# Offsets modulo 256 bytes of the matmul operands in a fused attention and MLP kernel

## The chip, the cores and the metric

The kernel runs on one core of a Trainium2 chip. The metric is the device time of one execution in microseconds (us). Of the kernel before there are three runs: 1198.25, 1200.48 and 1200.82 us, with a median of 1200.48 us.

## The reference

The input x has 2048 rows of 576 columns. It is normalised row by row (layer norm without weights), and three terms are added:

```python
xn = layernorm(x)
qkv = xn @ wqkv                      # 576 x 1728: 32 heads of 18
# each row attends to 8 keys: itself and 7 earlier rows, 2 apart
attn = softmax(q . k[idx] * 18**-0.5, masked where idx < 0)
A = (attn . v[idx]) @ wo             # 576 x 576
B = relu(xn @ w1) @ w2               # w1 576 x 4608, w2 4608 x 576
out = x + A + B
```

All of it is float32.

## The kernel before, in words

**Precision.** [...] Each operand is split into a high part (a rounded copy, ScalarE) and a low part (the rest, VectorE; `hi_lo`, line 278), and high times high, high times low and low times high are summed in PSUM. So each weight and activation tile has a high and a low half.

**Work and order.** The rows are taken in two phases of 1024 rows (`NPH`), each in two halves h of 512 rows. In a phase the 4608 columns of w1 are passed in 18 steps of 256; a step m has its own set of weights, and a half of a step is a unit g. Each unit computes h = relu(w1-columns x xn) for 512 rows and adds h times the rows of w2 to the outputs.

- *First product* (`classic`, line 583, and `pstep`, line 605): the weights of w1 (`wset`) are the stationary operand, 128 x 128, and the activations `xa`, `xs` (sums and differences of row blocks, in a scheme that saves one of eight block products) and `xr` (the last 64 rows of the contraction) the moving one, 256 wide, into the PSUM banks `bk2`, `bk3` and `bkA`. The steps P1 to P7 of a unit have six or eight matmuls each.
- *Output product* (`o_step`, line 720): 128 columns of `hhi` or `hlo` are the stationary operand and a row block of w2 (`w2t`) the moving one, in two pieces: 256 and 320 wide. Six matmuls, three pairs of 256 and 320, make one row block. The bank is `po`. The same function multiplies the turned attention output (`ohi`, `olo`) by wo; that tile comes from the pool `v`, whose two slots also hold the attention's values.
- *QKV* (`qkv_tile`, line 778): 14 matmuls a tile with the activations as stationary and a weight tile of 3 x 144 = 432 columns as moving operand, into `pm`. It uses the free one of the two weight buffers.

All matmuls but the transposes are issued in one helper (line 276), ScalarE's copies in another (line 270), VectorE's sums in a third (line 273). While one matmul streams its moving operand, the weights of the next are loaded from SBUF; the profile has the loads in a row of their own (PEld).

**Attention** runs on VectorE in the background, eight heads at a time, between the operations that TensorE waits for. The attention output is turned by way of DRAM.

**What sets the order.** The order of all instructions is written by the program: a planner (`Order`, line 55) keeps a clock for each engine, gives each ScalarE and VectorE operation a length and a due time, and issues the most urgent one that is ready. It knows nothing of addresses. Loads from DRAM are issued on SP's queue (`send`), with margins of some microseconds (`w2_make`, line 491: 4.0); copies of the weights within DRAM go on POOL's queue.

**Where tiles lie.** Each tile has 128 partitions; its offset in a partition follows from the order of the pools and of the tiles in them, each tile rounded up to 32 bytes. The pools are, in order, `keep` (the tiles that live for the whole run, the two weight buffers `BUF` among them), `w2p` (w2), `hp` (h), `whp` (turned attention output), `vp` (values and wo), `prp`, `lgp`, `smp` and `mvp` (scratch of attention and normalisation). A weight buffer has 10 x 432 floats, 17280 bytes. `wset` (line 247) cuts it into a high and a low half, 8640 bytes apart; `wqset` (line 251) into ten parts of 1728 bytes.

Of the kernel before, what the change touches and what calls it, by code (L numbers as in the profile page):

```python
# [9 lines left out]
F32 = mybir.dt.float32  # L10
F32R = mybir.dt.float32r
# [5 lines left out]
P = 128  # L17
NPH = 2
NI = 8
TBN = 256  # L20
W = 8
HG = 8
NU = 4
KT = 4
# [4 lines left out]
WOP = ((6, 9, 13, 16), (7, 10, 14, 17))  # L29
HALO = ((0, 112), (112, 127))  # L30
WARM = 24

S2, S4, S3, S1 = range(4)
T1, B11, T2, B21, T3, B22, T4, RR = range(8)
# [18 lines left out]
class Order:  # L53
# [82 lines left out]
    def act(self, fn, n, after, slack, lag=0.0):  # L136
        op = Op(ACT, n / 1120.0 + 0.06, fn, after, self.now() + slack, lag)
        self.wait[ACT].append(op)
        return op

    def dve(self, fn, n, after, slack, lag=0.0):
        op = Op(DVE, n / 960.0 + 0.062, fn, after, self.now() + slack, lag)
        self.wait[DVE].append(op)
        return op
# [6 lines left out]
    def send(self, fn, kb, after=(), margin=0.0):  # L151

        after = [a for a in after if a is not None]
        self.force(after)
        start = max([self.clk[SP], self.now() - 0.5] + [a.end for a in after])
        fn()
        op = Op(SP, 0.45, None, (), 0.0)
        self.clk[SP] = start + 0.45
        self.dma = max(self.dma, start + 0.3) + kb / 185.0
        op.end = max(start + 2.1, self.dma + 1.2) + margin  # L160
        return op
# [9 lines left out]
    def pe(self, fn, dur, after=()):  # L171
        after = [a for a in after if a is not None]
        self.force(after)
        start = max([self.clk[PE]] + [a.end for a in after])
        while self.step(start):
            pass
        fn()
        op = Op(PE, dur, None, (), 0.0)
        self.clk[PE] = start + dur
        op.end = start + dur + TAIL[PE]  # L180
        return op
# [8 lines left out]
def tile_body(ctx: ExitStack, tc: tile.TileContext, x, wqkv, wo, w1, w2, out):  # L190
# [4 lines left out]
    UD = HG * Dh  # L195
# [9 lines left out]
    ctx.enter_context(tc.manual_schedule())  # L205
    pool = lambda name, bufs, **k: ctx.enter_context(tc.tile_pool(name=name, bufs=bufs, **k))
    keep = pool("keep", 1)
    w2p = pool("w2p", 4)
    hp = pool("hp", 5)
    whp = pool("whp", 2)  # L210
    vp = pool("vp", 2)
    prp = pool("prp", 2)
    lgp = pool("lgp", 1)
    smp = pool("smp", 2)
    mvp = pool("mvp", 8)
    dram = pool("dram", 1, space=bass.MemoryType.DRAM)
    psp = pool("psp", 1, space=PSUM)

    f32 = lambda ap: ap.bitcast(F32)
# [10 lines left out]
    XA = [[keep.tile([P, 2, KT, TBN], F32R, name=f"xa{h}{j}") for j in range(2)] for h in range(2)]  # L230
    XS = [keep.tile([P, 2, 4, 2, TBN], F32R, name=f"xs{h}") for h in range(2)]
    XR = [keep.tile([P, 3, TBN], F32R, name=f"xr{h}") for h in range(2)]
    BUF = [keep.tile([P, 10 * 3 * UD], F32R, name=f"wset{b}") for b in range(2)]
    KK = keep.tile([P, W - 1 + NI, UD], F32, name="kk")
    TS = keep.tile([P, 4, 2, P], F32, name="ts")
    VV = {}
# [7 lines left out]
    bk3 = psp.tile([P, 512], F32, name="bk3")  # L244
    pm = psp.tile([P, 512], F32, name="pm")

    def wset(m):
        z = BUF[m % 2].rearrange("p (e c) -> p e c", e=2)[:, :, 0:2048]
        return z.rearrange("p e (s k c) -> p e s k c", s=8, k=2)

    def wqset(p):
        return BUF[(p + 1) % 2].rearrange("p (t c) -> p t c", t=10)

    def raw_view(z):
        v = z.rearrange("p w c -> p (w c)")[:, 0 : 8 * TBN].rearrange("p (j s k c) -> p j s k c", j=2, s=2, k=2)
        return [v[:, 0], v[:, 1]]

    KR = [raw_view(KK), raw_view(KK)]
    rr = [z.rearrange("p i c -> p (i c)")[:, 0 : 2 * TBN].rearrange("p (j c) -> p j c", j=2) for z in QO]
    RD = [rr[0][:, 0], rr[1][:, 0]]  # L260

    for _ in range(WARM):
        nc.tensor.transpose(po[0][:, 0, 0:P], ident, ident)
# [5 lines left out]
    def copy(o, i, func=AF.Copy):  # L269
        nc.scalar.activation(o, i, func)  # L270

    def sub(o, a, b, op=ALU.subtract):
        nc.vector.tensor_tensor(o, a, b, op=op)  # L273

    def mm(o, l, r, start, stop):
        nc.tensor.matmul(o, l, r, start=start, stop=stop, skip_group_check=True)  # L276

    def hi_lo(hi, lo, raw, n, after, slack):

        a = act(lambda: copy(hi, raw), n, after, slack)  # L280
        b = dve(lambda: sub(lo, raw, f32(hi)), n, [a], slack + 0.8)
        return [a, b]
# [60 lines left out]
    def place(i):  # L343
        return i // 4, i // 2 % 2, slice(i % 2 * P, (i % 2 + 1) * P)
# [68 lines left out]
    def slots_free(b, slots):  # L413
        f = SETFREE.get(b, {})
        return [f[q] for q in slots if q in f]
# [8 lines left out]
    def set_make(m, plain=False, fine=False):  # L424

        n = m % NP
        late = 0.0 if plain or fine or m == 2 else 4.0
        w = wset(m)
        z = f32(w)[:, 1]
        got = {}  # L430
# [65 lines left out]
    WQOK = {}  # L496

    def wq_make(p, u, kts, raw=None):

        w = wqset(p)  # L500
        b = (p + 1) % 2
        v = wqkv.rearrange("r (s c) -> r s c", s=3)[:, :, u * UD : (u + 1) * UD] if raw is not None else WQC[u]
        for kt in kts:
            z = raw[:, kt] if raw is not None else f32(w)[:, 5 + kt]
            after = [] if raw is not None else [kept["wq", u]]
            free = slots_free(b, range(432 * kt // 256, min(7, (432 * kt + 431) // 256) + 1))
            if raw is None:
                after += free
            z3 = z.rearrange("p (s c) -> p s c", s=3)
            if kt < KT:  # L510
                g = [send(lambda: nc.sync.dma_start(z3, v[kt * P : (kt + 1) * P]), 221, after)]
            else:
                g = [send(lambda rows=rows: nc.sync.dma_start(z3[rows], v[KT * P : D]), 110, after)
                     for rows in (slice(0, DR), slice(DR, P))]
            WQOK.setdefault(p, []).extend(hi_lo(w[:, kt], w[:, 5 + kt], z, 3 * UD, [*g, *free], 2.5))

    WO, WOOK = {}, {}

# [259 lines left out]
    def qkv_tile(p, u, i):  # L778
        ph = p // NP
        if i == 0:  # L780
            o_.force(KFREE[0])
            VV[u % 2] = vp.tile([P, W - 1 + NI, UD], F32, name="v")
            nc.gpsimd.memset(KK[0:1, 0 : W - 1, :], 0.0)
            nc.gpsimd.memset(VV[u % 2][0:1, 0 : W - 1, :], 0.0)
        k, v, q = KK, VV[u % 2], QO[u % 2]
        h, j, c = place(i)
        xa, wq = XA[h][j], wqset(p)
        o = pm[:, 0 : 3 * UD]
        lst = (
            [(xa[:, 0, kt, c], kt) for kt in range(KT)] + [(xa[:, 1, kt, c], kt) for kt in range(KT)]  # L790
            + [(XR[h][:, j, c], 4)] + [(xa[:, 0, kt, c], 5 + kt) for kt in range(KT)] + [(XR[h][:, j, c], 9)]
        )

        def f():
            for z, (l, b) in enumerate(lst):
                mm(o, l, wq[:, b], z == 0, z == len(lst) - 1)

        t = pe(f, 14 * 0.196, [*WQOK[p], *XOK[h, j], *BANK["pm"]])
        pq = o.rearrange("p (s c) -> p s c", s=3)

        def out_():
            copy(k[:, W - 1 + i, :], pq[:, 1])
            copy(v[:, W - 1 + i, :], pq[:, 2])
            copy(q[:, i, :], pq[:, 0])

        e = act(out_, 3 * (UD + 70), [t, *OFREE[u % 2]], 1.2)
        BANK["pm"] = [e]
        SETFREE[(p + 1) % 2] = {q: t for q in range(8)}
# [9 lines left out]
    def attention(ph, u, halo):  # L818
        qo, k, v = QO[u % 2], KK, VV[u % 2]
        heads = "p w (h d) -> p w h d"  # L820
        s = {}
        pr = {}

        def begin():
            s["lg"] = lgp.tile([P, NI, W, HG], F32, name="lg")
            s["m"] = smp.tile([P, NI, HG], F32, name="m")
            s["r"] = smp.tile([P, NI, HG], F32, name="r")

        def spread(z):
            return z[:, :, None, :].to_broadcast([P, NI, W, HG])  # L830
# [87 lines left out]
        for i in range(0, NI, 2):  # L918
            for f in (qk_mul, qk_sum):
                for j in (i, i + 1):  # L920
                    z = add(lambda f=f, j=j: f(j), big, halo if first else (), 1.3 if f is qk_sum and j == NI - 1 else 0.0)
# [26 lines left out]
    for m in range(2, NPH * NP):  # L948
        g = 2 * m - 2
        p = m - 1  # L950
# [15 lines left out]
    for ph in range(NPH):  # L966
        for u, n in enumerate(QP[ph]):
            p = ph * NP + n
            g = 2 * p
# [8 lines left out]
        for u, n in enumerate(WOP[ph]):  # L978
            g = 2 * (ph * NP + n)
# [59 lines left out]
        RAWR.pop(h, None)  # L1039

    def x_home(h):
        KR[h] = raw_view(vp.tile([P, W - 1 + NI, UD], F32, name="v") if h else KK)

    for h in range(2):
        g = GP - 1 + h
        at(g - 1, 0, x_home, h)
        at(g - 1, 0, clear, h)
        w = (
            ((33, 14), (33, 15), (33, 16), (33, 17)), ((34, 1), (34, 3), (34, 5), (34, 7)),
            ((34, 8), (34, 10), (34, 14), (34, 16)), ((34, 12), (34, 18)),  # L1050
        ) if h == 0 else (
            ((34, 13), (34, 15), (34, 19), (34, 20)), ((34, 20), (34, 22), (35, 1), (35, 2)),
            ((35, 3), (35, 5), (35, 9), (35, 11)), ((35, 7), (35, 13)),
        )
# [21 lines left out]
    def x_first(i, q=None):  # L1076
        XLAST[i] = send(lambda: (q or nc.sync).dma_start(X[i], x_v[0, i]), 295)

    x_first(0)
    x_first(1, nc.scalar)  # L1080
    VV[0] = vp.tile([P, W - 1 + NI, UD], F32, name="v")
    ST0 = VV[0].rearrange("p w c -> p (w c)")[:, 0:1280].rearrange("p (s k c) -> p s k c", s=5, k=2)
    RAWS = ((B11, 0, 0), (B21, 256, 0), (RR, 512, 0), (B12, 0, 1), (B22, 256, 1))
    SETOK[0] = {}
# [24 lines left out]

    KFREE[0] = WQOK[0]  # L1110
    OFREE[0] = [*W2OK[0, 0], *W2OK[0, 1]]
    KR[0] = raw_view(vp.tile([P, W - 1 + NI, UD], F32, name="v"))
    KR[1] = [
        QO[1].rearrange("p i c -> p (i c)")[:, 0 : 4 * TBN].rearrange("p (s k c) -> p s k c", s=2, k=2),
        TS.rearrange("p s k c -> p (s k c)").rearrange("p (s k c) -> p s k c", s=2, k=2),
# [64 lines left out]
    for g in range(2, NG + 1):  # L1180
        ph, n, h = G[g] if g < NG else (NPH, 0, 0)
# [58 lines left out]
```

## Time and profile before

| | before |
|---|---|
| runs, median of three | 1200.48 us |
| the profiled execution | 1201.66 us |
| its span, first to last instruction | 1199.9 us |
| mean granted TensorE clock | 0.990 |
| instructions | 21930 |
| VectorE busy in the stretch of 500 us from 660 us on | 356.82 us |
| TensorE busy in the same stretch | 496.15 us |
| bytes read and written in DRAM | 96.01 and 36.50 MB |

The span runs from the first to the last instruction of the profiled execution; the time of the execution has 1.8 us more around it. A busy time is the time in which at least one instruction of the engine was under way. Matmuls overlap, so their mean duration is longer than the time from one start to the next. In a group's row stand the line of the code, the engine, the operation, what is written and read, the shape, the count, then the busy time, the mean duration in ns and the idle time before it with its cause. A row of the timeline has the start, the length, the engine, and how many instructions were merged.

### The profile page before, as it was taken

The numbers are of one execution on the slowest core, as the hardware profiler recorded it, in microseconds if no ns is written. First come the engines' busy times: TensorE is split into PE (matmuls) and PEld (weight loads), VectorE is DVE, ScalarE is ACT, GpSimd is POOL, SyncE is SP. The second block draws the span as 40 slices with busy tenths as digits, with TensorE's granted clock in tenths as the row PEclk, the third lists the DMA queues.
The fourth block names the chain that finished last, engine by engine and source line by source line (L and its number), as shares of the span: only waits on it lengthen the run. The fifth ranks groups of instructions, "written<-read, shape, count | busy, mean of one in ns | idle before, by whom it ended". The sixth has DMA issues, their size and how long they took to land.

```text
span 1199.9 us, 21930 instructions
## 1 busy us (share of the span) xinstructions
PE 1162.5 (97%) x8528; PEld 1140.0 (95%) x8528; DVE 826.4 (69%) x1533; ACT 743.0 (62%) x1658; POOL 64.2 (5%) x97
## 2 busy tenths in 40 slices
PE   7999999999988999999999999999999999999998
PEld 6899999999988999899999999999999999999998
DVE  7648978953988169774683299589925994399731
ACT  5548466655656466566686567476646665566663
POOL 2200200110011001000010000000000000000000
PEclk8999999999999999899999999999999999999999
DMA  6752441562245232333352222231322213221322
GB/s 197 218 139 69 150 106 56 161 170 84 68 148 158 42 92 83 120 78 88 120 173 93 71 66 58 44 103 44 89 54 85 71 52 72 83 59 56 80 66 89
DMA packets 133544, 115.60 MB, mean 96 GB/s; under 512 B 54128, under 2 KB 112240, under 8 KB 133120
## 3 DMA queue, kind: packets, MB, share of 16 engines
q1 hardware_dynamic: 128192, 85.00, 25.7%
q0 software_dynamic: 5104, 28.90, 7.5%
q8 instruction: 67, 1.10, 0.4%
q14 instruction: 37, 0.30, 0.1%
q10 hardware_dynamic: 144, 0.29, 0.1%
HBM read 96.01 MB, written 36.50 MB: 110 GB/s over the span
## 4 chain that ended last, share of the span: by engine, by line
PE 73%; DVE 12%; ACT 8%; issue 3%; DMA 3%; POOL 0%; SPq 0%; ACTq 0%; DVEq 0%; POOLq 0%
PE po L276 32%; PE bk L276 21%; PE pm L276 14%; PE bkA L276 5%; DVE wset L273 3%; ACT po L270 2%; ACT x L270 2%; DVE ts L273 2%; DMA olo<-turned 1%; DVE hlo L554 1%; ACT wset L270 1%; DVE sn L273 1%; ACT hhi L270 1%; DVE pr L870 1%; DVE pr L840 1%
## 5 line engine op out<-in xcount | busy, mean ns | idle before, releaser
L276 PE MATMUL po<-w2t,hhi 128*128 128x256 f32 (+1 forms) x2304 | 407.1, 299 | 6.1 <-ACT po L270 5.9
L276 PEld LDWEIGHTS po<-w2t,hhi 128*128 128x128 f32 x2304 | 341.0, 190 | 10.9 <-ACT po L270 9.7
L276 PE MATMUL po<-w2t,hlo 128*128 128x256 f32 (+1 forms) x1152 | 248.1, 297 | 0.0
L276 PE MATMUL bk<-xs,wset 128*128 128x256 f32 x1632 | 238.2, 282 | 7.0 <-DVE sn L273 7.0
L270 ACT ACTIVATE x<-po 128x576 f32<-128x576 f32 x286 | 182.2, 644 | 100.3 <-PE po L276 97.6
L276 PEld LDWEIGHTS bk<-xs,wset 128*128 128x128 f32 x1632 | 217.7, 189 | 8.1 <-DVE sn L273 7.8
L276 PEld LDWEIGHTS po<-w2t,hlo 128*128 128x128 f32 x1152 | 195.7, 191 | 0.0
L270 ACT ACTIVATE po<-x 128x576 f32<-128x576 f32 x286 | 187.0, 654 | 2.9
L276 PE MATMUL pm<-wset,xa 128*128 128x432 f32 x768 | 172.9, 360 | 2.6 <-ACT wset L270 1.5
L276 PEld LDWEIGHTS pm<-wset,xa 128*128 128x128 f32 x768 | 140.2, 188 | 9.9 <-ACT qo L270 2.3
L276 PE MATMUL bk<-xa,wset 128*128 128x256 f32 x924 | 138.7, 288 | 7.5 <-DVE hlo L554 4.8
L273 DVE TENSOR_TENSOR sn<-bk,sn 128x256 f32<-128x256 f32 x136 | 57.2, 421 | 122.0 <-PE bk L276 81.2
L276 PEld LDWEIGHTS bk<-xa,wset 128*128 128x128 f32 x924 | 125.8, 193 | 13.2 <-DVE hlo L554 10.1
L273 DVE TENSOR_TENSOR w2t<-w2t 128x576 fp32r<-128x576 f32 (+1 forms) x72 | 54.1, 751 | 70.1 <-ACT w2t L270 69.4
L270 ACT ACTIVATE hhi<-sn 128x256 fp32r<-128x256 f32 x136 | 56.4, 415 | 72.7 <-DVE sn L273 72.7
L270 ACT ACTIVATE kk<-pm 128x144 f32<-128x144 f32 (+1 forms) x68 | 21.0, 308 | 114.6 <-PE pm L276 114.4
L870 DVE TENSOR_TENSOR pr<-lg,v 128x1152 f32<-128x1152 f32 x64 | 85.1, 1352 | 0.2
L276 PE MATMUL bk<-xr,wset 128*128 128x256 f32 x426 | 85.1, 281 | 0.0
L840 DVE TENSOR_TENSOR pr<-qo,kk 128x1152 f32<-128x1152 f32 x64 | 85.0, 1351 | 0.0
L843 DVE TENSOR_REDUCE lg<-pr 128x64 f32<-128x1152 f32 x64 | 84.8, 1345 | 0.0
L273 DVE TENSOR_TENSOR wset<-wset 128x512 fp32r<-128x512 f32 (+2 forms) x120 | 70.8, 599 | 11.9 <-ACT wset L270 11.5
L276 PE MATMUL bkA<-xa,wset 128*128 128x256 f32 x480 | 68.9, 281 | 2.0 <-DVE xr L273 2.0
(132 smaller groups left out, 1365.5 us busy)
## 6 DMA issues: line engine op xcount, KB each, us to landing
w2t<-w2c SPq DMA_DIRECT2D x70, 288.0 KB, 2.8
wset<-w1c SPq DMA_DIRECT2D x106, 128.0 KB, 2.4
w1c<-in_w POOLq DMA_DIRECT2D x18, 576.0 KB, 8.4
w2c<-in_w POOLq DMA_DIRECT2D x18, 576.0 KB, 8.8
wset<-wqc SPq DMA_DIRECT2D x28, 216.0 KB, 2.5
out<-x SPq DMA_DIRECT2D x16, 288.0 KB, 2.2
wset<-w1c SPq DMA_DIRECT2D x70, 64.0 KB, 2.2
ts<-w1c SPq DMA_DIRECT2D x34, 128.0 KB, 2.7
```

The costliest lines, as they stand in the source:

```text
L270: nc.scalar.activation(o, i, func)
L273: nc.vector.tensor_tensor(o, a, b, op=op)
L276: nc.tensor.matmul(o, l, r, start=start, stop=stop, skip_group_check=True)
L554: nc.vector.scalar_tensor_tensor(lo, src, 0.0, f32(hi), op0=ALU.max, op1=ALU.subtract)
L840: nc.vector.tensor_tensor(pr[i], q, window(k, i), op=ALU.mult)
L843: nc.vector.tensor_reduce(s["lg"][:, i], pr.pop(i).rearrange(heads, d=Dh), axis=AX.X, op=ALU.add)
L870: nc.vector.tensor_tensor(pr[i].rearrange(heads, d=Dh), e, window(v, i).rearrange(heads, d=Dh), op=ALU.mult)
```

## The change

The change moves tiles and pads strides. The arithmetic, the instructions on TensorE and their order in the program stay as they are.

1. Four pads (`PADS`, in floats: 16, 16, 32, 32, that is 64, 64, 128, 128 bytes) are put ahead of the weight buffers, of w2, of h with the turned attention output, and of `vp`. Nothing writes or reads them.
2. A weight buffer becomes [128, 2, 2176] floats: its halves are 8704 bytes apart, the two buffers 17408 bytes. The ten QKV parts become five in each half.
3. A tile of `vp` becomes 2176 floats (8704 bytes) in place of 2160 (8640); views cut it to the old shape.
4. To make room, `mvp` goes from 8 to 6 buffers, and `m` and `r` of the attention from 2 to 1.

The offsets modulo 256 bytes, worked out from the sizes of the tiles:

| tile | role | before | after |
|---|---|---|---|
| `xa`, `xs`, `xr` | moving in the first product, stationary in QKV | 192 | 192 |
| `wset`, even m: high, low half | stationary in the first product | 192, 128 | 0, 0 |
| `wset`, odd m: high, low half | the same | 64, 0 | 0, 0 |
| `w2t` | moving in the output product | 128 | 0 |
| `hhi`, `hlo` | stationary in the output product | 128 | 128 |
| `ohi`, `olo` | stationary for wo | 128 | 128 |
| `v` slots (wo) | moving for wo | 128 and 64 | 0 and 0 |

Offsets within a tile that the matmuls use (multiples of 512 or 1024 bytes, 2304 for the low half of w2 and wo) are multiples of 256, but for the QKV parts, 1728 bytes each.

```diff
+PADS = (16, 16, 32, 32)
...
     keep = pool("keep", 1)
+    pad1 = pool("pad1", 1).tile([P, PADS[1]], F32, name="pad1")
     w2p = pool("w2p", 4)
+    pad2 = pool("pad2", 1).tile([P, PADS[2]], F32, name="pad2")
     hp = pool("hp", 5)
     whp = pool("whp", 2)
+    pad3 = pool("pad3", 1).tile([P, PADS[3]], F32, name="pad3")
     vp = pool("vp", 2)
...
-    mvp = pool("mvp", 8)
+    mvp = pool("mvp", 6)
...
-    BUF = [keep.tile([P, 10 * 3 * UD], F32R, name=f"wset{b}") for b in range(2)]
+    keep.tile([P, PADS[0]], F32, name="pad0")
+    BUF = [keep.tile([P, 2, 2176], F32R, name=f"wset{b}") for b in range(2)]
...
+    def v_tile():
+        return vp.tile([P, 2176], F32, name="v")[:, 0 : (W - 1 + NI) * UD].rearrange("p (w c) -> p w c", w=W - 1 + NI)
+
     def wset(m):
-        z = BUF[m % 2].rearrange("p (e c) -> p e c", e=2)[:, :, 0:2048]
+        z = BUF[m % 2][:, :, 0:2048]
         return z.rearrange("p e (s k c) -> p e s k c", s=8, k=2)
 
     def wqset(p):
-        return BUF[(p + 1) % 2].rearrange("p (t c) -> p t c", t=10)
+        return BUF[(p + 1) % 2][:, :, 0 : 5 * 3 * UD].rearrange("p e (t c) -> p e t c", t=5)
...
-            VV[u % 2] = vp.tile([P, W - 1 + NI, UD], F32, name="v")
+            VV[u % 2] = v_tile()
...
-                mm(o, l, wq[:, b], z == 0, z == len(lst) - 1)
+                mm(o, l, wq[:, b[0], b[1]], z == 0, z == len(lst) - 1)
...
-            s["m"] = smp.tile([P, NI, HG], F32, name="m")
-            s["r"] = smp.tile([P, NI, HG], F32, name="r")
+            s["m"] = smp.tile([P, NI, HG], F32, name="m", bufs=1)
+            s["r"] = smp.tile([P, NI, HG], F32, name="r", bufs=1)
```

The other lines of the diff follow from these: the indices of the QKV parts, and `v_tile()` wherever a value tile was taken.

More of the change, by code (lines that the diff above doesn't have):

```diff
@@ L503, in wq_make @@
         for kt in kts:
-            z = raw[:, kt] if raw is not None else f32(w)[:, 5 + kt]
+            z = raw[:, kt] if raw is not None else f32(w)[:, 1, kt]
             after = [] if raw is not None else [kept["wq", u]]
@@ L514, in wq_make @@
                      for rows in (slice(0, DR), slice(DR, P))]
-            WQOK.setdefault(p, []).extend(hi_lo(w[:, kt], w[:, 5 + kt], z, 3 * UD, [*g, *free], 2.5))
+            WQOK.setdefault(p, []).extend(hi_lo(w[:, 0, kt], w[:, 1, kt], z, 3 * UD, [*g, *free], 2.5))
     WO, WOOK = {}, {}
@@ L789, in qkv_tile @@
         lst = (
-            [(xa[:, 0, kt, c], kt) for kt in range(KT)] + [(xa[:, 1, kt, c], kt) for kt in range(KT)]
-            + [(XR[h][:, j, c], 4)] + [(xa[:, 0, kt, c], 5 + kt) for kt in range(KT)] + [(XR[h][:, j, c], 9)]
+            [(xa[:, 0, kt, c], (0, kt)) for kt in range(KT)] + [(xa[:, 1, kt, c], (0, kt)) for kt in range(KT)]
+            + [(XR[h][:, j, c], (0, 4))] + [(xa[:, 0, kt, c], (1, kt)) for kt in range(KT)] + [(XR[h][:, j, c], (1, 4))]
         )
@@ L1041, in x_home @@
     def x_home(h):
-        KR[h] = raw_view(vp.tile([P, W - 1 + NI, UD], F32, name="v") if h else KK)
+        KR[h] = raw_view(v_tile() if h else KK)
     for h in range(2):
@@ L1080, in tile_body @@
     x_first(1, nc.scalar)
-    VV[0] = vp.tile([P, W - 1 + NI, UD], F32, name="v")
+    VV[0] = v_tile()
     ST0 = VV[0].rearrange("p w c -> p (w c)")[:, 0:1280].rearrange("p (s k c) -> p s k c", s=5, k=2)
@@ L1111, in tile_body @@
     OFREE[0] = [*W2OK[0, 0], *W2OK[0, 1]]
-    KR[0] = raw_view(vp.tile([P, W - 1 + NI, UD], F32, name="v"))
+    KR[0] = raw_view(v_tile())
     KR[1] = [
```

## The prediction

> **What bounds the kernel now.** I began with the page's busy times, the clock and the chain that ended last.
>
> ```profile
> PE 1162.5 (97%) x8528; PEld 1140.0 (95%) x8528; DVE 826.4 (69%) x1533; ACT 743.0 (62%) x1658; POOL 64.2 (5%) x97
> PEclk8999999999999999899999999999999999999999
> PE 73%; DVE 12%; ACT 8%; issue 3%; DMA 3%; POOL 0%; SPq 0%; ACTq 0%; DVEq 0%; POOLq 0%
> ```
>
> TensorE is the bound: 97% busy at nearly full clock and 73% of the chain. The weight load stream is busy 95% as well, so nearly all the time TensorE reads two things from SBUF at once: the moving operand of one matmul and the weights of the next. The change moves just these two against each other, so I then asked how many matmuls of each shape there are (groups by form, TensorE).
>
> ```profile
> L276 PE MATMUL po<-w2t,hhi 128*128 128x320 f32 x1152 | 335.1, 313 | 0.0
> L276 PE MATMUL bk<-xs,wset 128*128 128x256 f32 x1632 | 238.2, 282 | 7.0 <-DVE sn L273 7.0
> L276 PE MATMUL po<-w2t,hlo 128*128 128x320 f32 x576 | 179.8, 312 | 0.0
> L276 PE MATMUL pm<-wset,xa 128*128 128x432 f32 x768 | 172.9, 360 | 2.6 <-ACT wset L270 1.5 <-ACT qo L270 1.1
> L276 PE MATMUL bk<-xa,wset 128*128 128x256 f32 x924 | 138.7, 288 | 7.5 <-DVE hlo L554 4.8 <-ACT xa L270 2.0
> L276 PE MATMUL bk<-xr,wset 128*128 128x256 f32 x426 | 85.1, 281 | 0.0
> L276 PE MATMUL bkA<-xa,wset 128*128 128x256 f32 x480 | 68.9, 281 | 2.0 <-DVE xr L273 2.0
> L276 PE MATMUL pm<-wset,xr 128*128 128x432 f32 x128 | 45.7, 357 | 0.0
> L276 PE MATMUL po<-v,ohi 128*128 128x320 f32 x144 | 41.2, 310 | 0.0
> L276 PE MATMUL bkA<-xr,wset 128*128 128x256 f32 x148 | 29.4, 280 | 0.0
> L276 PE MATMUL po<-v,olo 128*128 128x320 f32 x60 | 18.6, 311 | 0.0
> L276 PE MATMUL po<-v,w2t 128*128 128x320 f32 x20 | 5.5, 309 | 0.0
> ```
>
> Each 320-wide row has a 256-wide twin, so they count pairs: 1152+576 = 1728 pairs with w2, 144+60+20 = 224 with wo. The other groups are 1632+924+426+480+148 = 3610 matmuls of the first product and 768+128 = 896 of QKV. A mean duration of 280 to 360 ns is latency; what counts is the time from one start to the next, which the timeline gives.
>
> The trace already holds an experiment on offsets, since two pairs of buffers differ by 128 or 192 bytes modulo 256. I write "apart" for the weights' offset less the moving operand's, modulo 256. **First, wo.** It lies in the `v` buffers at 128 or at 64; `ohi` and `olo` lie at 128. Starts of twelve matmuls with the slot at 128 (0 apart):
>
> ```profile
> 244.87 0.70 PE L276 MATMUL po<-v,ohi 128*128 128x256 f32 x4
> ...
> 246.21 0.43 PE L276 MATMUL po<-v,olo 128*128 128x256 f32 x2
> 246.47 0.28 PE L276 MATMUL bk<-xa,wset 128*128 128x256 f32 x1
> ```
>
> and with the slot at 64 (64 apart):
>
> ```profile
> 487.73 0.69 PE L276 MATMUL po<-v,ohi 128*128 128x256 f32 x4
> ...
> 489.05 0.43 PE L276 MATMUL po<-v,olo 128*128 128x256 f32 x2
> 489.32 0.28 PE L276 MATMUL bk<-xa,wset 128*128 128x256 f32 x1
> ```
>
> Five pairs take 246.21-244.87 = 1.34 us (268 ns a pair) at 0 apart and 489.05-487.73 = 1.32 us (264 ns) at 64 apart; all six, to the next group, 1.60 and 1.59 us (267 and 265). So the offset does act on TensorE's pace, by 2 to 4 ns in 267. I take 3.
>
> **Second, the first product.** The stages of even m have their weights at 192 (high) and 128 (low), those of odd m at 64 and 0; x is always at 192. An even and an odd stage, sixteen matmuls each (P4 of one half, P5 of the next):
>
> ```profile
> 701.67 0.87 PE L276 MATMUL bk<-xa,wset 128*128 128x256 f32 x6
> ...
> 703.55 0.30 PE L276 MATMUL po<-w2t,hhi 128*128 128x256 f32 x1
> ```
>
> ```profile
> 726.86 0.88 PE L276 MATMUL bk<-xa,wset 128*128 128x256 f32 x6
> ...
> 728.77 0.29 PE L276 MATMUL po<-w2t,hhi 128*128 128x256 f32 x1
> ```
>
> Even: 1.88 us / 16 = 117.5 ns a matmul. Odd: 1.91 / 16 = 119.4 ns. Of eight weight loads five are high and three low: in the odd stage five are 128 apart from x and three 64, in the even one five are 0 and three 192 apart.
>
> **The change, part by part.** No instruction of the computation is added or removed; the counts above stay.
>
> *w2 and h (1728 pairs).* From 0 apart (w2 128, h 128) to 128 apart (0 and 128). No 256/320 pair of the trace is 128 apart. Below, the nearest good row: 64 apart saves 3 ns. Above, the 256-wide matmuls that are mostly 128 apart are 1.9 ns slower than those mostly 0 apart; twice that a pair is +3.8 ns. The wo row is nearer, being the same shapes, bank and code (`o_step`): I take -3 ns, so 1728 x 3 = **-5.2 us** (ends -5.2 and +6.6 by these rows; a longer gain is a rival).
>
> *wo and the turned attention output (224 pairs).* Both `v` slots come to 0 with `ohi`, `olo` at 128. About half were 0 apart and gain the same 3 ns, the other half stay: 112 x 3 = **-0.3 us**. Twenty pairs at the end have w2's buffer as weights and come to 0 apart: 20 x 3 = 0.06 us lost, nothing.
>
> *The weight buffers in the first product (3610).* All weights come to 64 apart. That is the distance that wo shows as good, and the odd stages hold it in only three of eight. I take that the odd half (1805) gains half of the 1.9 ns between the two stages, and that the even half stays: 1805 x 1 = **-1.8 us**. Ends: all at the even stage's pace or better by as much again (-1.9 x 3610 = -6.9) and all at the odd one's (+1.9 x 1805 = +3.4).
>
> *QKV (896).* Here the weight buffer is the moving operand, in parts of 1728 bytes, which step by 192 modulo 256; the parts lie at four offsets before and after, in another order. I count **0**; a shift of 1.5 ns a matmul either way, about the size seen above, would be 1.3 us.
>
> *Buffers cut to make room.* `m` and `r` are written and read by VectorE alone, in its own order, so one buffer adds no wait on another engine. `mv` and `rstd` go from 8 to 6: the seventh normalisation waits for what the first read, six row blocks earlier. Cost 0; if that cover were gone, TensorE's transposes would stand behind the waiting VectorE, and the longest wait of that kind bounds it:
>
> ```profile
> PE bk L337 <- DVE mv L308: 2.2, 1, 2.2
> ```
>
> so +2.2 us at most. The pads are tiles that nothing writes: no instruction, no DMA. The DMAs keep their sizes and counts; those into w2 land in 2.8 us of median, and the planner puts their users 4 us behind the landing that it expects (the margin in `w2_make`), so other start addresses in SBUF cost nothing unless a landing comes some 4 us later.
>
> ```profile
> w2t<-w2c SPq DMA_DIRECT2D x70, 288.0 KB, 2.8
> ```
>
> *What is late next.* A faster TensorE runs into the engines that feed it. One stage of steady state, with attention in the background:
>
> ```profile
> 690.30:715.40 25.10, 24.77 (x198) 24.53 (x196) 22.93 (x35) 17.21 (x36) 0.00 (x0) 1.00 0.20 60
> ```
>
> TensorE is busy 24.77 of 25.10 us and VectorE 22.93 (91%), so a per cent fits, 9% would not. TensorE carries 73% of the chain overall and 99% here; I let 80% of the saving through.
>
> **Sum:** (-5.2 - 0.3 - 1.8) x 0.8 = -7.3 x 0.8 = -5.8 us. The profiled execution took 1201.66 us (span 1199.9 and 1.8 around it): 1195.8. It lies 1.2 us above the median of 1200.48, so **1194.6**, said as 1195 us.
>
> **Rivals.**
>
> *The gain is larger.* At 128 and 64 apart both streams could settle at the shortest pace seen anywhere. The even stage's P3 took
>
> ```profile
> 699.14 0.87 PE L276 MATMUL bk<-xs,wset 128*128 128x256 f32 x6
> ...
> 700.07 0.70 PE L276 MATMUL po<-w2t,hhi 128*128 128x256 f32 x4
> ```
>
> 0.93 us / 8 = 116.3 ns. All first products at that: (118.4 - 116.3) x 3610 = -7.6 us, 118.4 being the mean of the two stages. Pairs at twice the step of wo: -6 x 1728 = -10.4 us. Together -18 x 0.9 = -16: 1184. For it: the distances are uniform afterwards, no matmul meets a bad one. Against: no row shows a whole stage that fast.
>
> *Slower: 128 apart is the bad distance.* The odd stages' high products are 128 apart and are the slowest of the trace. If pairs follow them, each loses 3.8 ns: +6.6 us, and if 64 apart brings the first product nothing, this stands alone: 1200.5 + 6.6 x 0.9 = 1206.5. It decides as soon as a w2 pair takes more than 267 ns. Against it: wo, of the same shapes, gains by leaving 0 apart.
>
> *Nothing moves.* Gains in the pairs and losses in the first product cancel, or VectorE's 91% swallows the rest, or the unwritten pads get no room, so that w2 and h stay 0 apart: 1200 +- 2. By wo's row the first needs 128 apart to be within 1.4 ns of 0 apart (2.4 us / 1728 pairs). The Trainium skill, page "SBUF — State Buffer", section "Who interferes with whom", gives TensorE two independent read ports, one for the moving operand and one for the weights, and lets only the port pair of VectorE and GpSimd cause contention; by it offsets change nothing and the time stays at 1200.5. The trace disagrees: 268 against 264 ns for the same pairs at two offsets.
>
> **How the numbers follow.** Forecast (1191 to 1198): 0.38. Larger gain (1178 to 1191): 0.20. Nothing moves: 0.17. Slower (1203 to 1212): 0.25. A measurement of this kernel tells some 0.2%, 2.4 us, from no change. Faster is 0.38 + 0.20 = 0.58, same 0.17, slower 0.25. For 8 in 10 the range leaves out a tenth at either end: the lower half of the larger gain, below 1182, and slower than 1209, where the bounds of pairs and first product (+6.6 + 3.4 = +10, let through by 0.9) would add up. On the faster side alone it is 1182 to 1198.
>
> **What would show it.** Right: pairs of w2 at 264 ns in the timeline, the 320-wide group's mean down from 313 to about 310; even and odd stages of the first product alike at 117 to 118 ns; QKV groups as they are; no new wait of TensorE in the list of waits. Wrong: w2 pairs at 267 or more; first products at 119; a saving in the starts that comes back as idle time of TensorE after VectorE or ScalarE; DMA landings of w2 near 7 us.

## The result, and the profile after

| | before | after |
|---|---|---|
| runs, median of four each (before: one more beside after) | 1200.65 us | 1188.23 us |
| lowest and highest | 1198.25, 1201.97 | 1187.59, 1192.76 |
| the profiled execution, its span | 1201.66, 1199.9 | 1192.76, 1191.0 |
| mean granted TensorE clock | 0.990 | 0.990 |

The kernel after is faster: the ratio of the times is 0.9907, with a 95% interval of 0.9878 to 0.9936. That is 12.4 us by the medians. The profiled execution of after was the slowest of its four, so the two traces, compared below, differ by less: 8.9 us of span.

First the page of after: busy times, clock, and the engines' shares of the chain that ended last.

```profile
PE 1146.5 (96%) x8528; PEld 1120.7 (94%) x8528; DVE 825.1 (69%) x1533; ACT 742.1 (62%) x1658; POOL 64.4 (5%) x97
PEclk9999999999989999899999999999999999999999
PE 67%; DVE 18%; ACT 5%; DMA 5%; issue 3%; SPq 1%; POOL 0%; DVEq 0%; ACTq 0%; POOLq 0%
```

TensorE's busy time fell by 16 us with the same 8528 instructions at the same clock; VectorE's and ScalarE's stayed. But TensorE's share of the chain fell from 73 to 67%, and VectorE's rose from 12 to 18%: something now ends later than TensorE more often. Next the groups by form of after (columns as before: count, busy time, mean duration in ns, idle time before and its cause).

```profile
L284 PE MATMUL po<-w2t,hhi 128*128 128x320 f32 x1152 | 327.9, 306 | 0.0
L284 PE MATMUL bk<-xs,wset 128*128 128x256 f32 x1632 | 234.3, 279 | 11.3 <-DVE sn L281 11.3
L284 PE MATMUL po<-w2t,hlo 128*128 128x320 f32 x576 | 176.2, 306 | 0.0
L284 PE MATMUL pm<-wset,xa 128*128 128x432 f32 x768 | 172.9, 360 | 2.7 <-ACT wset L278 1.6 <-ACT qo L278 1.1
L284 PE MATMUL po<-v,ohi 128*128 128x320 f32 x144 | 40.6, 305 | 0.0
```

The 320-wide matmuls with w2 went from 313 and 312 to 306, those with wo from 310 to 305; the first product's from 282 to 279; QKV stayed at 360. The starts say it without the latency. The timeline of TensorE in after, one stage of steady state (start, length, merged count):

```profile
696.64 0.68 PE L284 MATMUL po<-w2t,hhi 128*128 128x256 f32 x4
...
698.20 0.85 PE L284 MATMUL bk<-xa,wset 128*128 128x256 f32 x6
...
699.12 0.84 PE L284 MATMUL bk<-xs,wset 128*128 128x256 f32 x6
```

Six pairs with w2 take 698.20-696.64 = 1.56 us, 260 ns a pair. The eight first products behind them take 699.12-698.20 = 0.92 us, 115 ns each. The same step of the next stage, whose weights lie in the other buffer:

```profile
722.88 0.85 PE L284 MATMUL bk<-xa,wset 128*128 128x256 f32 x6
...
723.80 0.94 PE L284 MATMUL bk<-xs,wset 128*128 128x256 f32 x6
```

723.80-722.88 = 0.92 us again: the difference between even and odd stages is gone.

**A tally of all starts.** TensorE runs the same matmuls in the same order in both kernels, so I compared the traces start by start. A step, from one start to the next, counts as one with a wait when in either trace it is more than 80 ns longer than the median of its kind. The steps without a wait lost 20.2 us in sum, those with one gained 11.3 us; together that is the difference of the spans, -8.9 us. Mean times from one start to the next, waits left out:

| | before, ns | after, ns | times the count |
|---|---|---|---|
| first product, even stages | 117.6 | 114.8 | |
| first product, odd stages | 118.5 | 114.8 | |
| first product, all 3610 | 118.0 | 114.8 | -11.7 us |
| w2, 256 wide and 320 wide, 1728 pairs | 118.1 + 148.6 | 119.1 + 142.3 | -9.1 us |
| wo, 224 pairs | 117.9 + 147.6 | 118.8 + 143.4 | -0.7 us |
| QKV, 896 | 196.2 | 196.7 | +0.4 us |

(These products sum to -21.1; they count every matmul, and the tally of 20.2 leaves out the steps with a wait. The means move by up to about half a nanosecond with how waits are told apart.)

**What took half of it back.** The list of TensorE's waits in before (engine, tile waited for, releaser; total us, times, longest):

```profile
PE bk L276 <- DVE sn L273: 7.0, 4, 2.9
PE po L276 <- ACT po L270: 6.3, 12, 1.9
PE bk L276 <- DVE hlo L554: 4.8, 13, 0.8
```

and in after:

```profile
PE bk L284 <- DVE sn L281: 11.3, 4, 5.1
PE po L284 <- ACT po L278: 7.4, 13, 2.0
PE bk L284 <- DVE hlo L562: 6.0, 17, 0.8
PE bk L284 <- ACT xa L278: 3.1, 1, 3.1
```

The last row stood at 2.0 before. These four sum to 20.1 and 27.8 us: +7.7 of the +11.3. The largest is `sn`, four waits in both, the longest grown from 2.9 to 5.1. To see what stands behind that one I followed the chain back from there, first in before:

```profile
342.93 8.22 DMA olo<-turned
...
351.17 0.42 ACT ohi L270
...
352.38 1.27 DVE pr L870
353.65 0.35 DVE sn L273
```

and in after:

```profile
340.18 10.40 DMA olo<-turned
...
350.60 0.42 ACT ohi L278
...
351.81 1.27 DVE pr L878
353.07 0.35 DVE sn L281
```

The turned attention output comes back from DRAM; ScalarE's copy `ohi` stands in its queue until it has landed; VectorE takes `olo`, a piece of attention (`pr`), and only then `sn`, the sum that TensorE wants. The landing came at 342.93+8.22 = 351.15 before and at 340.18+10.40 = 350.58 after. TensorE's timeline around it, before and then after:

```profile
350.92 0.39 PE L276 MATMUL bk<-xr,wset 128*128 128x256 f32 x2
354.04 0.97 PE L276 MATMUL bk<-xs,wset 128*128 128x256 f32 x6 [2.73 <-DVE sn L273]
```

```profile
347.99 0.39 PE L284 MATMUL bk<-xr,wset 128*128 128x256 f32 x2
353.46 1.65 PE L284 MATMUL bk<-xs,wset 128*128 128x256 f32 x6 [5.08 <-DVE sn L281]
```

TensorE arrived 350.92-347.99 = 2.93 us earlier and went on 354.04-353.46 = 0.58 us earlier. What it had won up to there was wiped out but for 0.6 us. The same wait near 490 us grew from 2.85 to 4.01 us.

The load itself was issued 342.93-340.18 = 2.75 us earlier and took 10.40 us instead of 8.22. The stretch from 343 to 347 us, before and then after (the last two numbers are the DMA engines' busy share and GB/s):

```profile
343.00:347.00 4.00, 4.00 (x34) 3.96 (x33) 3.93 (x7) 2.69 (x6) 0.00 (x0) 1.00 1.05 349
```

```profile
343.00:347.00 4.00, 4.00 (x34) 4.00 (x33) 1.71 (x4) 0.00 (x0) 0.00 (x0) 1.00 1.01 341
```

In both the DMA engines were fully busy while the load was on its way. So it may have stood among other transfers that a faster TensorE doesn't shorten; that is a reading of the trace, which no run tests.

### The profile page after: what moved, and what is told of

Its sections match the earlier page's. It is cut to its first block, busy times and chain, and to the rows that moved or that the text cites. A ratio compares the mean times of both kernels' runs of the same rounds, so it can differ in the third digit from the quotient of the medians.

```text
span 1191.0 us, 21930 instructions
## 1 busy us (share of the span) xinstructions
PE 1146.5 (96%) x8528; PEld 1120.7 (94%) x8528; DVE 825.1 (69%) x1533; ACT 742.1 (62%) x1658; POOL 64.4 (5%) x97
## 4 chain that ended last, share of the span: by engine, by line
PE 67%; DVE 18%; ACT 5%; DMA 5%; issue 3%; SPq 1%; POOL 0%; DVEq 0%; ACTq 0%; POOLq 0%
PE po L284 28%; PE bk L284 19%; PE pm L284 14%; PE bkA L284 5%; DVE wset L281 3%; DVE ts L281 2%; DVE hlo L562 2%; DVE pr L878 2%; DMA olo<-turned 2%; DVE sn L281 1%; DVE pr L885 1%; ACT x L278 1%; ACT po L278 1%; ACT wset L278 1%; DMA wset<-wqc 1%
## 5 line engine op out<-in xcount | busy, mean ns | idle before, releaser
L284 PE MATMUL po<-w2t,hhi 128*128 128x256 f32 (+1 forms) x2304 | 401.5, 296 | 7.5 <-ACT po L278 7.0
L284 PEld LDWEIGHTS po<-w2t,hhi 128*128 128x128 f32 x2304 | 334.8, 189 | 14.0 <-ACT po L278 11.6
L284 PE MATMUL po<-w2t,hlo 128*128 128x256 f32 (+1 forms) x1152 | 245.4, 294 | 0.0
L284 PE MATMUL bk<-xs,wset 128*128 128x256 f32 x1632 | 234.3, 279 | 11.3 <-DVE sn L281 11.3
L284 PEld LDWEIGHTS bk<-xs,wset 128*128 128x128 f32 x1632 | 213.3, 189 | 12.4 <-DVE sn L281 12.0
L284 PEld LDWEIGHTS po<-w2t,hlo 128*128 128x128 f32 x1152 | 191.5, 189 | 0.0
L284 PEld LDWEIGHTS bk<-xa,wset 128*128 128x128 f32 x924 | 123.3, 192 | 16.5 <-DVE hlo L562 11.9
L278 ACT ACTIVATE kk<-pm 128x144 f32<-128x144 f32 (+1 forms) x68 | 21.0, 309 | 114.8 <-PE pm L284 114.6
L281 DVE TENSOR_TENSOR wset<-wset 128x512 fp32r<-128x512 f32 (+2 forms) x120 | 70.8, 599 | 12.4 <-ACT wset L278 12.2
L885 DVE TENSOR_TENSOR pr<-pr 128x288 f32<-128x288 f32 (+1 forms) x128 | 70.5, 600 | 0.0
```

Of the source, the lines that this page charges most:

```text
L885: nc.vector.tensor_tensor(o, z[:, 0:n], z[:, n : 2 * n], op=ALU.add)
```

## The experiments

I kept four theories apart. **Distance:** what counts is how far the weights lie from the moving operand within one group (first product, or output product), as the prediction had it. **Absolute:** what counts is that a moving operand begins at a multiple of 256 bytes, as w2 does after and not before. **Rhythm:** the matmuls fall into one of several paces that repeat themselves, and what chooses among them is the offsets of all that TensorE reads one after the other, the group just before included; then the parts of the change don't add up. And, for what is given back, **VectorE:** it is too busy to follow a faster TensorE.

All runs in one table. "Apart" is weights less moving operand, modulo 256, in the first product and in the w2 pairs; the third column says how w2, h and wo lie together against x and the weight buffers, taken from where after has them (only kernels in which the two distances are those of after can be compared by it). Paces are means of the times from start to start, in ns, waits left out, tallied from the trace of each kernel's profiled execution; the column of w2 takes the first two pairs of each three (1152), the table above took all 1728. Ratios go against the kernel before on the same chip (1200.7 to 1201.5 us); where there is none, there was one execution only.

| kernel | first product apart | w2 pairs apart | shift of w2, h, wo | time, us | ratio [95%] | first product | w2 pair |
|---|---|---|---|---|---|---|---|
| before | 0, 192 / 128, 64 | 0 | | 1200.65 | | 118.0 | 266.9 |
| after | 64 | 128 | 0 | 1188.23 | 0.9907 [0.9878, 0.9936] | 114.8 | 261.1 |
| po_only | as before | 128 | | 1197.77 | 0.9980 [0.9965, 0.9994] | 117.7 | 265.5 |
| bk_only | 64 | 0 | | 1200.91 | 0.9997 [0.9987, 1.0007] | 117.5 | 266.8 |
| grid_0_64 | 0 | 64 | | 1206.03 | | 119.3 | 266.1 |
| grid_128_192 | 128 | 192 | | 1198.39 | | 118.6 | 263.9 |
| shift64 | 64 | 128 | 0 | 1189.39 | 0.9909 [0.9888, 0.9930] | 114.9 | 261.3 |
| group64 | 64 | 128 | 64 | 1196.75 | 0.9965 [0.9951, 0.9979] | 116.7 | 263.1 |
| group128 | 64 | 128 | 128 | 1190.18 | 0.9915 [0.9889, 0.9940] | 115.3 | 264.7 |
| group192 | 64 | 128 | 192 | 1188.38 | 0.9890 [0.9865, 0.9916] | 114.5 | 261.2 |
| bk192_po128 | 192 | 128 | | 1193.89 | 0.9936 [0.9921, 0.9951] | 117.4 | 262.9 |
| po160 | 64 | 160 | | 1199.17 | | 117.7 | 266.3 |

### Each part alone

**po_only:** the kernel before with one pad, so that h and the turned attention output come to 0 while w2 stays at 128.

```diff
+    pad2 = pool("pad2", 1).tile([P, 32], F32, name="pad2")
     hp = pool("hp", 5)
```

> The kernel before with one pad of 128 bytes ahead of h alone: w2 stays at 128 and h comes to 0, so pairs of w2 are 128 apart as in the changed kernel, and w2 itself does not begin at a multiple of 256. The weight buffers, and wo's distances (0 and 64), stay as before. Theory D (only the distance between the next weights and the moving operand counts): pairs of w2 at 260 ns as in the changed kernel, first product at 117.5 and 119.4 ns as before, time 1191 to 1195 us. Theory A (what counts is that the moving operand begins at a multiple of 256): pairs stay at 267 ns, time 1200 us.

1197.77 us in ten runs, 0.2% faster. The pairs lie 128 apart as in after and yet take 265.5 ns on the mean, not 261: the commonest are 260 ns (288 of the 1152), 270 (171), 269 (135) and 267 (103). The distance lets the short pair occur and doesn't make it the rule.

**bk_only:** the kernel before with the weight buffers as in after. All that lies behind them moves along by 64 bytes, w2 and h together, which stay 0 apart.

```diff
+    keep.tile([P, 16], F32, name="pad0")
-    BUF = [keep.tile([P, 10 * 3 * UD], F32R, name=f"wset{b}") for b in range(2)]
+    BUF = [keep.tile([P, 2, 2176], F32R, name=f"wset{b}") for b in range(2)]
```

> The kernel before with the weight buffers of the changed kernel alone (strides 8704 and 17408 bytes, 64 bytes of pad ahead, 6 mv buffers to make room). All weights of the first product are 64 apart from x; w2 and h stay 0 apart from each other. Theory D: first product at 114 to 115 ns in even and odd stages, pairs at 267 ns, time 1192 to 1197 us. If what TensorE saves came through in full, this part alone would give 3610 x 3.3 = 12 us and the pairs alone 1728 x 6.5 = 11 us; the two parts together gave 12 us by the medians, so the rival theory V (VectorE and ScalarE take back what TensorE saves) expects each part alone to give more than half of the whole, 7 to 10 us.

1200.91 us: nothing. Its timeline, the step that took 115 ns a matmul in after:

```profile
702.27 0.87 PE L277 MATMUL bk<-xa,wset 128*128 128x256 f32 x6
...
704.16 0.70 PE L277 MATMUL po<-w2t,hhi 128*128 128x256 f32 x4
```

Sixteen matmuls (of `xa`, `xr`, `xs` and `xr`) in 704.16-702.27 = 1.89 us: 118.1 ns each, at the very distance of after. So after's 115 ns don't come from the distance in the first product alone. The two parts give 0.2% and nothing, and together 0.9%: they don't add up, which speaks against Distance and for Rhythm. (The cut to `m` and `r` and the new stride of `vp`, with wo's new distance, are in neither part.)

### Other distances, and all tiles moved together

**grid_0_64** and **grid_128_192** are after with other pads; w2 begins at a multiple of 256 in both.

```diff
-PADS = (16, 16, 32, 32)
+PADS = (0, 32, 16, 48)
```

> The changed kernel with other pads: weights 0 apart from x in the first product, w2 and wo at 0 as in the changed kernel, h and the turned output at 64, so pairs are 64 apart. Theory D: first product near 117.5 to 119 ns, pairs at 264 ns as wo had them in the kernel before at 64 apart, time 1195 to 1199 us. Theory A: pairs at 260 ns, since w2 begins at a multiple of 256 still; time about 1194 us.

```diff
-PADS = (16, 16, 32, 32)
+PADS = (32, 0, 48, 16)
```

> The changed kernel with other pads: weights 128 apart from x in the first product, w2 and wo at 0, h and the turned output at 192, so pairs are 192 apart. Theory D: first product at 119 to 122 ns, the slow side; pairs unknown, between 260 and 267 ns; time 1198 to 1207 us. Theory A: pairs at 260 ns, time about 1195 us.

grid_0_64, 0 and 64 apart, came out slower than the kernel before (one execution; the highest of 19 of the kernel before on that chip was 1204.50 us). TensorE's timeline:

```profile
697.92 0.88 PE L283 MATMUL bkA<-xa,wset 128*128 128x256 f32 x6
...
698.88 0.88 PE L283 MATMUL bk<-xs,wset 128*128 128x256 f32 x6
699.60 0.70 PE L283 MATMUL po<-w2t,hhi 128*128 128x256 f32 x4
...
700.40 0.70 PE L283 MATMUL po<-w2t,hhi 128*128 128x256 f32 x4
```

698.88-697.92 = 0.96 us for eight first products, 120 ns each. Here 0 apart is slow, where the prediction feared 128; yet before's even stages, 0 apart in five of eight, took 117.6. Three pairs take 700.40-699.60 = 0.80 us, 267 ns each, with w2 at 0 as in after: Absolute falls, since w2's beginning alone gives nothing. At 64 apart wo had taken 264 to 265 ns in before's trace; that doesn't carry over to w2 either. grid_128_192, 128 and 192 apart, took 1198.39 us; its first products ran in a cycle of five steps that repeats itself, 115, 118, 122, 120 and 119 ns or within 1 ns of that (mean 118.6), its pairs mostly at 262 to 265. No one distance in the first product stands out as good: 64 apart, the best in after, gave 118 in bk_only.

**shift64** is after with 64 bytes ahead of x, so that everything moves and every distance stays.

```diff
+    keep.tile([P, 16], F32, name="padx")
```

> The changed kernel with one more pad of 64 bytes ahead of x's tiles, so that x, the weight buffers, w2, h, the turned output and wo all begin 64 bytes further on and every distance between them stays. Theory A (multiples of 256 count): w2 now begins at 64 and the weights at 64, the gain goes, 1197 to 1201 us. Theory D (distances within a group count) and theory R (see the next runs): the same as the changed kernel, 1188 us, pairs at 260 ns and first product at 115 ns.

1189.39 us and 114.9 and 261.3 ns: as after, though w2 now begins at 64. That settles it against Absolute. Only offsets against each other count.

### The two groups against each other

**group64, group128, group192** move w2, h and wo together against x and the weight buffers. Both distances within the groups stay those of after.

```diff
-PADS = (16, 16, 32, 32)
+PADS = (16, 32, 32, 32)
```

> The changed kernel with w2, h, the turned output and wo all moved by 64 bytes against x and the weight buffers: within the first product the distance stays 64, within the pairs 128; only the distances across the joints move (first h after x: from 192 to 0 apart; first weights after w2: from 0 to 192). Theory D: as the changed kernel, 1188 us. Theory R (a run of matmuls settles into one of several rhythms that repeat themselves, and the joints and what went before choose which): the first product may stand at 113 or at 117.5 ns and the pairs at 260 or 267 ns with the same distances; time anywhere from 1187 to 1201 us, and not all three of group64, group128 and group192 alike.

```diff
-PADS = (16, 16, 32, 32)
+PADS = (16, 48, 32, 32)
```

> As group64, with w2, h, the turned output and wo moved by 128 bytes: distances within the first product 64, within the pairs 128, as in the changed kernel; joints 64 apart (h after x) and 128 apart (weights after w2). Theory D: 1188 us. Theory R: one of the rhythms, 1187 to 1201 us, with the first product at 113 or 117.5 ns and the pairs at 260 or 267 ns.

```diff
-PADS = (16, 16, 32, 32)
+PADS = (16, 0, 32, 32)
```

> As group64, with w2, h, the turned output and wo moved by 192 bytes: distances within the first product 64, within the pairs 128; joints 128 apart (h after x) and 64 apart (weights after w2). Theory D: 1188 us. Theory R: one of the rhythms, 1187 to 1201 us, with the first product at 113 or 117.5 ns and the pairs at 260 or 267 ns.

group64 loses two thirds of the gain (1196.75 us; 0.9965, its interval clear of after's), with nothing changed but where one group, and the attention's scratch behind it, lie against the other. Its timeline:

```profile
695.54 0.68 PE L284 MATMUL po<-w2t,hhi 128*128 128x256 f32 x4
...
697.10 0.87 PE L284 MATMUL bk<-xa,wset 128*128 128x256 f32 x6
...
698.99 0.77 PE L284 MATMUL po<-w2t,hhi 128*128 128x256 f32 x4
```

The pairs take 697.10-695.54 = 1.56 us for six, 260 ns, as in after. The first products behind them take (698.99-697.10)/16 = 118.1 ns, not 115. To count the paces I took the 357 runs of at least six first products with no other matmul between, and of each the pace from its fourth start to its sixth. In after 284 runs went at 113 to 114 ns and 55 at 117.5 to 118.5; in group64 116 and 218; in bk_only 28 and 303; in group128 312 and 30; in group192 293 and 41. There are two paces, with little between, at one and the same distance of 64.

What TensorE did just before has a part in the choice, and after shows it by itself. Two rows of first products of after, 5 us apart, each with the next QKV row:

```profile
665.80 0.87 PE L284 MATMUL bk<-xa,wset 128*128 128x256 f32 x6
...
667.68 1.74 PE L284 MATMUL pm<-wset,xa 128*128 128x432 f32 x8
...
671.25 0.85 PE L284 MATMUL bk<-xa,wset 128*128 128x256 f32 x6
671.94 1.72 PE L284 MATMUL pm<-wset,xa 128*128 128x432 f32 x8
```

The sixteen from 665.80 on come right behind QKV and take (667.68-665.80)/16 = 117.5 ns each; the six at 671.25 come behind w2 and take (671.94-671.25)/6 = 115. Over the whole trace, where nothing was waited for, 238 of the 264 runs behind w2 went at the short pace and 19 of the 21 behind QKV at the long one. In light_after (below), where VectorE works on less, it is 244 of 265 and 20 of 21, at the same two paces; so the operations left out there don't explain it. Distance, as the prediction used it, falls as the whole account; Rhythm is what remains, as a description.

group128 and group192 are as fast as after within the intervals. No version was clearly faster than after.

**bk192_po128** puts the weight buffers 192 from x, with w2 at 128 and h at 0.

```diff
-PADS = (16, 16, 32, 32)
+PADS = (48, 16, 32, 32)
```

> The changed kernel with the weights 192 apart from x in the first product; pairs 128 apart; w2 at 128, h at 0, so the joints are 64 apart (h after x) and 0 apart (weights after w2). Theory D: the first product takes what the even stages' low halves showed in the kernel before, near 117 ns, time 1192 to 1196 us. Theory R: a rhythm of its own, not to be told beforehand, 113 to 120 ns; if 113 ns with pairs at 260 ns, 1183 to 1189 us, the best of all.

1193.89 us, some 60% of the gain (7.6 of 12.4 us): pairs mostly at 260 ns (583 of the 1152; 270 ns 186 times), first products at 117.4.

**po160** moves h by 32 bytes, from 128 to 160.

```diff
-PADS = (16, 16, 32, 32)
+PADS = (16, 16, 40, 24)
```

> The changed kernel with h and the turned output at 160 in place of 128: pairs are 160 apart, a step of 32 bytes. If offsets count in steps of 64 bytes, the pairs run at 260 ns as at 128 apart or at 264 as at 192 apart, nothing else; if finer steps count, at another pace between 257 and 270 ns. Time 1187 to 1200 us.

1199.17 us, one execution: 2.3 us below the kernel before on the same chip, so most of the gain is gone. Its timeline:

```profile
697.93 0.70 PE L284 MATMUL po<-w2t,hhi 128*128 128x256 f32 x4
...
699.53 0.87 PE L284 MATMUL bk<-xa,wset 128*128 128x256 f32 x6
...
701.41 0.70 PE L284 MATMUL po<-w2t,hhi 128*128 128x256 f32 x4
```

Pairs: (699.53-697.93)/6 = 267 ns. First products: (701.41-699.53)/16 = 117.5 ns, though nothing about x and the weight buffers was touched. So, in this execution, 32 bytes in one operand of the output product decide about both groups.

### What takes the gain back

**light_before** and **light_after** are the two kernels without the weighted sum of the values (`av_mul`, `av_add`), on VectorE in the background of attention.

```diff
-        for i in range(0, NI, 2):
-            for j in (i, i + 1):
-                add(lambda j=j: av_mul(j), big)
-            for w in (4, 2, 1):
-                for j in (i, i + 1):
-                    add(lambda j=j, w=w: av_add(j, w), w * UD)
```

> The kernel before without the weighted sum of the values: the 64 multiplications and 192 additions of VectorE that turn the attention weights into the attention output are left out (85.1 + 46.2 + 26.4 + 16.9 = 174.6 us of VectorE), so q is turned in place of the attention output. Pairs and first products keep the pace of the kernel before (267 ns; 117.5 and 119.4 ns). Theory V (VectorE takes back part of what TensorE saves): some waits of TensorE for VectorE go, time 1185 to 1198 us. Rival: time within 0.3% of 1200.7 us.

> The changed kernel without the weighted sum of the values (as light_before). Theory V: with VectorE free the saving of TensorE comes through, and light_after is faster than light_before by more than the changed kernel is faster than the kernel before (12 us): by 16 to 22 us. Rival (the rest is lost elsewhere: on ScalarE, on loads, or is no saving at all): the difference stays at 10 to 13 us.

1206.73 us (1.0043, 1.0027 to 1.0060) and 1193.02 us (0.9926, 0.9912 to 0.9941). They differ by 13.7 us by the medians, 1.3 us more than before and after, which the intervals don't tell from no difference. VectorE was busy for 670.0 and 669.5 us instead of 826.4 and 825.1, and yet a faster TensorE kept little more of its gain, if any, by this measure. The profiled executions differ by more, 1204.1-1189.7 = 14.4 us of span against 8.9, but the one of after was the slowest of its four. So VectorE's load is not the main price; a part of it stays open. And taking the work out made the kernel before slower. ScalarE's waits for the turned attention output, before, after, light_before and light_after in this order (total us, times, longest):

```profile
ACT ohi L270 <- DMA olo<-turned: 14.3, 5, 5.6
```

```profile
ACT ohi L278 <- DMA olo<-turned: 17.3, 4, 7.7
```

```profile
ACT ohi L270 <- DMA olo<-turned: 29.5, 6, 10.2
```

```profile
ACT ohi L278 <- DMA olo<-turned: 30.3, 5, 11.0
```

The wait grew from before to after and doubled in the light kernels, where VectorE had less to do. The planner writes another order when operations are missing, so these two kernels don't show VectorE's share by itself. That the copy `ohi` blocks ScalarE until the transfer has landed is what the chain shows; a kernel with that copy placed later was not run.

## Why the prediction was right, and where its sum went wrong

The sign held, and so did the first half of the mechanism: TensorE bounds the kernel, and the offsets act on its pace. The second half, that the distance within a group sets the pace, did not hold alone. The time, 1188.2, lies within the range, but outside the forecast's own 1191 to 1198 and inside the larger gain's band. The saving on TensorE was mis-sized by a factor of nearly three, -7.3 us against some -21, and the share let through was too high; that the two errors partly cancel is luck. By its steps:

- *w2 and h, -5.2 us.* 128 apart was a gain, as chosen, but wo's 3 ns was the wrong size: a step of 5.3 ns a pair, -9.1 us. The short pair, 260 ns, is a rhythm that wo's row at 64 apart didn't show.
- *wo, -0.3 us.* -0.7.
- *First product, -1.8 us.* **This is the term that was mis-sized most: -11.7 us.** The step that failed is "I take that the odd half (1805) gains half of the 1.9 ns between the two stages, and that the even half stays". Both halves came to 114.8 ns. (The 1.9 ns came from one even and one odd stage; over the whole trace of before the two differ by 118.5-117.6 = 0.9 ns.) Half a nanosecond was right for what was reasoned about, the distance alone: bk_only went from 118.0 to 117.5. The rest came only with the other edits, through what runs before each group, which no step of the prediction had: it added up parts that don't add up.
- *QKV, 0.* 196.2 to 196.7 ns, 0.4 us.
- *Cut buffers, 0.* Right, as far as the sign that was named for it shows. The wait that was to show it, in the list of after, is as long as it was:

```profile
PE bk L345 <- DVE mv L316: 2.2, 1, 2.2
```

- *DMAs into w2, 0.* Right; the median landing is that of before:

```profile
w2t<-w2c SPq DMA_DIRECT2D x70, 288.0 KB, 2.8
```

- *What is late next, 0.8 let through.* Too much. Of 20.2 us, 8.9 came through between the two traces, 0.44; by the medians 12.4, about 0.6 if the other runs of after had the trace's pace. And the reason was looked for in the wrong place: at the longest wait it isn't VectorE's 91% that ended last, but a transfer whose landing hardly moved, with operations of ScalarE and VectorE in line behind it. "No new wait of TensorE" was wrong in size, not in kind: the same four `sn` waits, 7.0 to 11.3 us.
- *Larger gain, 1184.* Nearest in pace: it had first products at 116.3 (114.8 measured) and 6 ns a pair (5.3). Its 0.9 let through was too much as well; two errors that partly cancel.
- *Slower: 128 apart is the bad distance.* Refuted for the pairs; 0 apart in the first product with 64 in the pairs (grid_0_64, one execution) was what came out slower.
- *Nothing moves.* Refuted: the same matmuls took 1188 to 1206 us with nothing but pads changed (after, group64, grid_0_64). The Trainium skill, page "SBUF — State Buffer", section "Who interferes with whom", lets only the port pair of VectorE and GpSimd cause contention. What the prediction drew from it, that offsets change nothing, is wrong here; whether TensorE's two reads hold each other up is not shown.

Open is why there are two paces, 113 and about 118 ns, and by what means one is chosen. The runs show that relative offsets, also across groups and, in one execution, down to 32 bytes, and the kind of matmuls just before decide; they don't show the mechanism. Open too is what holds up the transfer.

## What to carry to other kernels

Where both of TensorE's reads, moving operand and weights, are busy all the time, the offsets of the tiles modulo 256 bytes are worth a try of their own: pads alone moved this kernel between 1188 and 1206 us. Try whole layouts and measure each, rather than add up the parts; the pace from start to start, by group, tells in one profile whether a layout is good. Then look for what doesn't move with TensorE, here a transfer by way of DRAM with a copy waiting on it in ScalarE's order, since that gives part of the gain back.

## What was not expected of the hardware

- One shape at one distance has two paces that repeat themselves: 113 to 114 ns in 284 runs of the first product and 117.5 to 118.5 ns in 55 (after), 116 and 218 (group64).
- What TensorE did just before acts on the pace of a group: within after, the short pace in 238 of 264 runs behind w2 and the long one in 19 of 21 behind QKV. And it depends on how the groups' tiles lie against each other: first products at 115 and 118 ns behind the same 260 ns pairs (after, group64).
- A step of 32 bytes in the weights of one group cost about 10 us (po160, one execution, 2.3 us below before where after lies 12.4 below), with the pairs at 266.3 ns where after has 261.1.
- A short 320-wide step is paid for in part by the 256-wide one: 148.6 to 142.3 ns and 118.1 to 119.1 ns.
